# Release point of held outputs, buffers of the last batch and the order of the opening in a one-core attention-and-convolution kernel

## The chip, the cores and the metric

The kernel runs on one core of a Trainium2 chip. The metric is the device time of one execution in microseconds (us). The kernel before has three timed runs, 1046.08, 1042.27 and 1046.51 us, so a median of 1046.08 us, and one profiled execution of 1042.6 us.

## The reference, cut to what matters

```
# u, v: (8, 3136, 256)   z: (8, 3136, 64)   B, S, D = 8, 3136, 256
scores = z @ z.T / S
attn   = maximum(scores, 0) ** 2
x      = u * (attn @ v)
x1, x2, x3 = split(x @ w_proj)                       # three times 256 columns
conv   = irfft(rfft(x2, axis=1) * rfft(filter, axis=0), n=S, axis=1)
out    = (x1 * conv * x3) @ w_out
```

Inputs and output are float32. The convolution is circular, along the 3136 positions, each of 256 channels by itself.

## The kernel before, in words

**Tiles.** The 3136 positions are seen as 64 times 49 (N1 times N2). They make 25 tiles of 128 positions, the last half full, in seven chunks of 512, 384, 512, 384, 512, 384 and 448 positions (CHUNKS). The eight batches follow each other, seven chunks each.

**Attention.** For each pair of position tiles (a "unit") and each chunk, TensorE makes scores into PSUM (score_mm, L1335), ScalarE applies the relu (L1510), and the square is made by VectorE (L1519) or ScalarE (L1517), whichever the planner finds earlier. The weighing matmuls (L1365; L1472 for the half tile) multiply the squares by v and sum in PSUM. Scores are symmetric, so a square made for one chunk is also used for the next two: DMA transposes on SyncE's queue (L1450) write it to the tiles M, M2e, M2o. VectorE then multiplies by u (L1559), for which u comes in by GpSimd DMA and is transposed by SyncE's queue (L1196).

**Projection and convolution.** Each chunk is projected. Two products become a gate (L897, L909, L917), kept in SBUF; the third (L940) goes through the first part of a Fourier transform (dft1, L755) and is put to DRAM (D1, L762). When a batch has all its chunks there, its 16 lines are loaded (load_spec, L787), transformed (forward, L808 and L816), multiplied by the filter's spectrum H on VectorE (L1012), transformed back (inverse or inverse2), and put to DRAM again (D2, L1062). Then add_end loads each chunk (load_c, L799), does the last part (L1098, L1101), multiplies by the gate (L1104), by w_out (L1132), copies to an output tile (copy, L359 on ScalarE or L363 on VectorE) and stores it (L1160, two DMAs for a chunk).

**The end of the kernel.** In the last batch a load_spec brings two lines instead of four, and from a ring of two buffers (l_p). The four chunks 3 to 6 of batch 6 are held back (HOLD is 3): their ends are of the planner's lowest kind, FZ, and may start once the last square of batch 7 (q_) is made. Their inputs and three of their output tiles lie in memory that v's buffers leave (cut_in, cut_out). The ends of batch 7 go in the order FINAL (0, 2, 4, 6, 1, 3, 5) and write to R_p tiles (two buffers) for even chunks, then xh_p tiles (three buffers) for odd ones.

**The opening.** z of batch 0 is loaded in three pieces by SyncE's queue (L450, ten DMAs), cast twice side by side by VectorE or ScalarE (L363, L359), turned by TensorE (L551) and copied to zT. v comes by GpSimd's queue in three pieces (L418, L423). Small tables are made meanwhile, as one chain: constants per partition (percol, L590 to L595; percol2, L598 to L614, 17 instructions on 128x1), the table T1 (t1_first, sin_steps with lines L627, L628, L632, then a sine L635), its transpose (t4_pe, L660), and the table S2 (L678 to L685, then L695 to L703), with transposes of S2 (L717) at the end.

**What sets the order.** The kernel is scheduled by hand: a planner (class Plan) runs through a model of the engines with the costs that each task is given, and emits an instruction where its model starts it. Each engine's order, and each queue's, is then fixed. S (scores) come first; FA, W, FB and FZ fill the rest by credit. `after(task, at)` forbids the model to start a task before a time; ZF_AT, V_AT and U_AT are such times, for pieces of z, v and u. A dependence marked ISSUED orders only the model and adds no wait on the chip. So a changed time in the opening moves instructions in all eight batches.

Of the kernel before, what the change touches and what calls it, by code (L numbers as in the profile page):

```python
# [11 lines left out]
P = 128  # L12
F32 = mybir.dt.float32
BF16 = mybir.dt.bfloat16
# [229 lines left out]
def kernel(  # L244
# [108 lines left out]
    def on(engine, emit, cost, deps=(), takes=(), **kw):  # L353
        return job(None, lambda e: emit(), {engine: cost}, deps, takes, **kw)
# [117 lines left out]
    wp16 = const.tile([P, 2, 3 * D], BF16, name="wp16")  # L472
    nc.gpsimd.dma_start(out=wp16[:], in_=moe_w_proj.rearrange("(t p) n -> p t n", p=P))
    wo16 = const.tile([P, 2, D], BF16, name="wo16")
    ZF_AT, V_AT, U_AT = (4.5, 6.0, 7.0), (8.0, 15.0), (19.0, 22.0)

    def filt_row(i, n=1):
        t = filt[i // 8]
# [135 lines left out]
        nc.vector.tensor_scalar(half, half, -0.5, 1.0, ALU.mult, ALU.add)  # L614

    step("DVE", percol, 0.9)

    def sin_steps(box, w, first, dst=None, at=0.0):
        def a():
# [31 lines left out]
        nc.vector.tensor_scalar(m[:, N1 : N1 + 1], k1v[:, 0:1], n1p, pb, ALU.mult, ALU.add)  # L651

    t1_done, _ = sin_steps({}, P, t1_first, T1[:, :], 6.6)
    step("DVE", percol2, 2.6)

    box1 = {}

# [15 lines left out]
    for j0 in (0, 8):  # L673
        box = {}

        def first(m, j0=j0):
            if j0:
                nc.vector.scalar_tensor_tensor(php, tp, 8.0, php, ALU.mult, ALU.add)  # L678
            nc.vector.tensor_scalar(m[:, 0 : 8 * N2], k2v, tp, php, ALU.mult, ALU.add)

        def masks(j0=j0, box=box):
            v = box["v"][:KR, 0 : 8 * N2].rearrange("p (j k) -> p j k", k=N2)
            a = int(j0 == 0)
            nc.vector.tensor_scalar(S2[:KR, ds(3 + j0 + a, 8 - a), 0:N2], v[:, a:], r0[:KR], None, ALU.mult)
            nc.vector.tensor_scalar(S2[:KR, ds(3 + j0, 8), 50 : 50 + N2], v, r1[:KR], None, ALU.mult)  # L685

        _, ta = sin_steps(box, 8 * N2, first)
        t = step("DVE", masks, 0.8)
        t.frees.append((ta, 0))
        if j0 == 0:  # L690
            join(t, s2_zero)
        s2_done.append(t)
# [86 lines left out]
    def by_row(d):  # L779
        return d[0:S, :].rearrange("(p x) d -> p x d", x=2 * NJ)  # L780

    def load_spec(src, j0, nj, deps, late=0.0):
        box = {}

        def go():
            box["t"] = l_p.tile()
            nc.sync.dma_start(out=box["t"][:KR, 0 : 2 * nj, :], in_=by_row(src)[:, ds(2 * j0, 2 * nj), :])  # L787

        t = on("SP", go, 0.45, [*deps, *((d, ISSUED) for d in loads[-1:])], [l_p.slots], moves=0.6 * nj, late=late)
        return in_order(t), box  # L790

    def load_c(src, c, deps, home):
# [88 lines left out]
    def add_proj(b, c, xt, xt_tasks):  # L881
# [83 lines left out]
            to_spectrum()  # L965
        return users, puts, gtasks

    def add_spectrum(b, puts):
        deps0 = list(h_done) + list(tz_done) if b == 0 else []
        final = b == B - 1  # L970
# [4 lines left out]
        for g in range(NJ // 2):  # L975
            own = not final or g % 2 == 0
            xh, gh = (xh_p, gs_p) if own else (R_p, A_p)
            if 2 * g % per == 0:
                ldb[0] = load_spec(D1[b % 2], 2 * g, per, puts, LATE_LOAD * (not final))
            ld, ibox = ldb[0]  # L980
            ends_load = (2 * g + 2) % per == 0
            xb = {}
            evs = []
            firsts = []
            for i in range(2):
                j = 2 * g + i
                box = {}

                def mm(i=i, j=j, box=box, xb=xb, ibox=ibox, xh=xh):
                    box["p"] = bank()  # L990
                    if i == 0:
                        xb["x"] = xh.tile([P, 2, 4, D], BF16)
                    x = ibox["t"][:KR, ds(2 * (j % per), 2), :].rearrange("p c d -> p (c d)")
                    forward(box["p"], x, j)

                def ev(e, i=i, box=box, xb=xb):
                    copy(e, xb["x"][:KC, 0, ds(2 * i, 2), :].rearrange("p c d -> p (c d)"), box["p"][:KC, :])

                a = pe("FB", mm, c_line(j), [ld, *deps0, *firsts], [ps_m.slots, *([] if i else [xh.slots])])
                firsts = [a]  # L1000
                if i == 0:
                    a0 = a
                elif ends_load:
                    a.frees.append((ld, 0))
                e_ = job(None, ev, both(2 * D), [a])
                e_.frees.append((a, 0))
                evs.append(e_)

            def mul(i, g=g, xb=xb):
                x = xb["x"][:KC].rearrange("p i (j c) d -> p i j c d", c=2)  # L1010
                h = H[:KC, ds(2 * g, 2), i].unsqueeze(2).to_broadcast([KC, 2, 2, D])
                nc.vector.tensor_tensor(x[:, 1 - i], x[:, 0], h, ALU.mult)  # L1012

            def add(xb=xb):
                x = xb["x"][:KC].rearrange("p i (j c) d -> p i c j d", c=2)
                nc.vector.tensor_tensor(x[:, 1, 0], x[:, 1, 0], x[:, 0, 1], ALU.subtract)
                nc.vector.tensor_tensor(x[:, 1, 1], x[:, 1, 1], x[:, 0, 0], ALU.add)

            cost = c_dve2(4 * D)
            w_ = on("DVE", lambda mul=mul: mul(0), cost, evs, prio=ZP)  # L1020
            w_ = on("DVE", lambda mul=mul: mul(1), cost, [w_], prio=ZP, lat=ZL)
            z_ = w_ if final else on("DVE", add, 2 * c_dve2(2 * D), [w_], prio=ZP)

            def inv(g=g, xb=xb, z_=z_, a0=a0, gh=gh):
                if 2 * g % per == 0:
                    gb[0] = {"es": [], "firsts": []}
                gx = gb[0]
                for i in range(2):
                    j = 2 * g + i
                    box = {}  # L1030
                    new = j % per == 0

                    def mm(j=j, box=box, new=new):
                        box["p"] = bank()
                        if new:
                            gx["g"] = gh.tile([P, 2 * per, D], BF16)
                        z, y = (xb["x"][:KC, i, ds(j % 2 * 2, 2), :].rearrange("p c d -> p (c d)") for i in range(2))
                        if final:
                            inverse2(box["p"], y, z, j)
                        else:  # L1040
                            inverse(box["p"], y, j)

                    def ev(e, j=j, box=box):
                        copy(e, gx["g"][:KR, ds(2 * (j % per), 2), :].rearrange("p c d -> p (c d)"), box["p"][:KR, :])

                    a = pe(
                        "FB", mm, c_line(j) * (1 + final), [z_, *gx["firsts"], *(minus_task if final else [])], [ps_m.slots] + ([gh.slots] if new else [])
                    )
                    gx["firsts"] = [a]
                    if new:  # L1050
                        gx["g0"] = a
                    if i:
                        a.frees.append((a0, 1))
                    e_ = job(None, ev, both(2 * D), [a])
                    e_.frees.append((a, 0))
                    gx["es"].append(e_)
                if (2 * g + 2) % per:
                    return
                j0 = 2 * g + 2 - per

                def put():
                    nc.sync.dma_start(  # L1062
                        out=by_row(D2[b % 2])[:, ds(2 * j0, 2 * per), :], in_=gx["g"][:KR, 0 : 2 * per, :]
                    )

                p_ = on("SP", put, 0.4, gx["es"], moves=0.5 * per, late=LATE_D2 * (not final))
                p_.frees.append((gx["g0"], 1))
                lasts.append(p_)

            behind.append(inv)  # L1070
            if g >= SPEC_LAG:
                behind.pop(0)()
# [2 lines left out]
        return lasts  # L1075

    def add_end(b, lasts, gtasks, cs, kind="FB", src=c_p, dsts=(o_p,), late=0, behind=(), then=(), split=False):
        for c in cs:
            t0, nt = T0[c], len(tiles[c])
            w = CHUNKS[c]  # L1080
            dst = dsts[c % len(dsts)]
            ld, cb = load_c(D2[b % 2], c, lasts, src)
            yb = {}
            ys = []
# [289 lines left out]
    def add_weigh(un, data, done):  # L1374
        global_k = len(plans[un[:2]])

        def part(dhs):
# [6 lines left out]
                [ps_o[dh].slots for dh in dhs] if k == 0 else [],  # L1384
            )
            if b == 0 and c == 0:
                after(t, V_AT[0] if max(plans[b, c][k][1]) < 7 else V_AT[1])
            if 1 in dhs:
                done(t)
            if k == 0:  # L1390
# [86 lines left out]
    for gi, g in enumerate(groups):  # L1477
# [22 lines left out]
        for i, un in enumerate(g):  # L1500
# [22 lines left out]
                "ACT", relu, c_act(n * cw), [(st, -sum(costs[i + 1 :]) - extra)], [R_p.slots], prio=0  # L1523
            )
            r_.frees.append((st, i))
            q_ = job(None, sq, both(n * cw, "DVE"), [r_], [A_p.slots], prio=1)
            q_.frees.append((r_, 0))
            if c == NC - 1 and last or gi == len(groups) - 1:
                if b == 0:
# [14 lines left out]
            if last:  # L1544
# [24 lines left out]
                if c == NC - 1:  # L1569
# [7 lines left out]
                        held = lasts, gts  # L1577
                        held_w = w_
                    else:
                        add_end(b, lasts, gts, FINAL, "FB", A_p, (R_p, xh_p), split=True)  # L1580
                        early = [*held[0], held_w]
                        outs = (o_p, cut_out, cut_out, cut_out, o_p, o_p)
                        add_end(b - 1, early, held[1], range(HOLD, NC), "FZ", cut_in, outs, 4, [(loads[-1], ISSUED)], [q_])
                    if b == 0:
                        hold = Held(v_p.slots, v_slot[0])
                        w_.frees.append((hold, 0))
# [58 lines left out]
```

## Time and profile before

| what | us |
|---|---|
| profiled execution | 1042.6 |
| its span, first to last instruction | 1040.7 |
| around the span | 1.9 |
| TensorE busy in the span | 989.8 |
| ScalarE busy | 912.6 |
| VectorE busy | 819.1 |
| GpSimd busy | 190.4 |
| mean granted TensorE clock | 0.992 |
| DMA moved in the span | 167.99 MB |

A row of a timeline has the start, the length, the engine, the line in the kernel, the operation with output and inputs, how many instructions are merged, and in brackets how long the engine was idle before and what released it. A row of the windows view gives, for a stretch, the busy time and the number of instructions of TensorE (PE), its weight loads (PEld), VectorE (DVE), ScalarE (ACT) and GpSimd (POOL), then the granted clock, the mean busy share of the 16 DMA engines, and GB/s. Merged matmuls overlap: their length is the sum of the steps from start to start and the last one's own length.

### The profile page before, as it was taken

How to read it: one execution, taken by the hardware profiler on the slowest of the kernel's cores; microseconds unless marked ns; L12 is line 12 of the kernel's file. 1: busy time of each engine (PE TensorE's matmuls, PEld its weight loads, DVE VectorE, ACT ScalarE, POOL GpSimd, SP SyncE). 2: the span in 40 equal slices, each digit the busy share in tenths (PEclk: the TensorE clock that was granted, in tenths of full speed). 3: DMA queues.
4: the chain of work that ended last, by engine and by line, in shares of the span. 5: the costliest groups of instructions: out<-in, count | busy, mean ns of one | idle time of the engine just before them, and what ended most of it. 6: DMA issues, size and time to landing. Idle time of an engine off the chain costs nothing.

```text
span 1040.7 us, 17903 instructions
## 1 busy us (share of the span) xinstructions
PE 989.8 (95%) x6010; PEld 480.7 (46%) x6078; DVE 819.1 (79%) x1497; ACT 912.6 (88%) x1273; POOL 190.4 (18%) x401
## 2 busy tenths in 40 slices
PE   5999899999999999999999999999999999999974
PEld 2444444444444545445454454444544454444553
DVE  6867588977788768986879777997879968897673
ACT  6998799987999889997999889997989989999672
POOL 5033111311023300313021311121202230001000
PEclk9999999999999999999999999999999999999997
DMA  9599767888887868899888979798887977868357
GB/s 165 96 157 180 136 141 147 164 147 164 184 159 138 170 135 206 167 153 145 160 203 156 172 170 181 147 173 157 193 174 147 161 167 163 201 137 184 83 157 214
DMA packets 324380, 167.99 MB, mean 161 GB/s; under 512 B 234088, under 2 KB 302184, under 8 KB 324288
## 3 DMA queue, kind: packets, MB, share of 16 engines
q1 hardware_dynamic: 296560, 135.87, 59.7%
q0 software_dynamic: 27728, 30.97, 21.7%
q8 instruction: 48, 0.79, 0.3%
q14 instruction: 44, 0.36, 0.1%
HBM read 90.26 MB, written 53.35 MB: 138 GB/s over the span
## 4 chain that ended last, share of the span: by engine, by line
PE 75%; DVE 8%; ACT 7%; DMA 5%; issue 3%; SPq 1%; another core or an unknown queue 0%; ACTq 0%; DVEq 0%; POOL 0%; POOLq 0%
PE ps_o_t L1365 40%; PE ps_s_t L1335 11%; PE ps_m_t L940 4%; ACT R_t L1510 4%; PE ps_m_t L1132 4%; PE ps_m_t L909 3%; PE ps_m_t L897 3%; PE ps_m_t L755 2%; DMA M_t<-A_t 2%; PE ps_m_t L824 2%; PE ps_m_t L1101 2%; PE ps_m_t L816 2%; DVE xT_t L1559 2%; DVE A_t L1519 2%; ACT A_t L1517 1%
## 5 line engine op out<-in xcount | busy, mean ns | idle before, releaser
L1510 ACT ACTIVATE R_t<-ps_s_t 128x1024 f32<-128x1024 f32 (+2 forms) x552 | 485.0, 921 | 33.3 <-PE ps_s_t L1335 27.8
L1365 PE MATMUL ps_o_t<-A_t,v_t 128*128 128x512 bf16 (+2 forms) x2011 | 465.4, 354 | 3.6 <-issue 0.5
L1365 PEld LDWEIGHTS <-v_t 128*128 128x128 bf16 x2688 | 253.6, 98 | 241.6 <-issue 30.0
L1519 DVE TENSOR_TENSOR A_t<-R_t 128x768 bf16<-128x768 f32 (+2 forms) x271 | 290.7, 1080 | 35.2 <-ACT R_t L1510 29.4
L1517 ACT ACTIVATE A_t<-R_t 128x768 bf16<-128x768 f32 (+3 forms) x281 | 265.8, 958 | 5.4 <-DMA spec<-s_t 0.9
L1335 PE MATMUL ps_s_t<-zT_t 64*128 64x512 bf16 (+2 forms) x1088 | 155.3, 358 | 3.7 <-ACT R_t L1510 3.0
L408 POOL COPY tick<-xT_t 1x1 bf16<-1x1 bf16 x54 | 15.9, 294 | 737.5 <-DVE xT_t L1559 737.5
L1559 DVE SCALAR_TENSOR_TENSOR xT_t<-ps_o_t,uT_t 128x256 bf16<-128x256 f32 (+1 forms) x224 | 76.5, 383 | 29.1 <-PE ps_o_t L1365 18.4
L917 DVE TENSOR_TENSOR gate_t<-ps_m_t,x_t 128x256 bf16<-128x256 f32 (+1 forms) x208 | 69.0, 385 | 30.8 <-PE ps_m_t L909 15.1
L1365 PE MATMUL ps_o_t<-M_t,v_t 128*128 128x384 bf16 (+2 forms) x336 | 79.1, 346 | 6.7 <-DMA M_t<-A_t 6.6
L1012 DVE TENSOR_TENSOR xh<-xh,H 100x1024 bf16<-100x1024 bf16 x120 | 81.5, 684 | 2.3 <-ACT xh L359 1.4
L1335 PEld LDWEIGHTS <-zT_t 64*128 64x128 bf16 x1088 | 32.9, 94 | 101.8 <-issue 99.8
L359 ACT ACTIVATE x_t<-ps_m_t 128x512 bf16<-128x512 f32 (+3 forms) x114 | 61.7, 564 | 16.7 <-PE ps_m_t L897 12.2
L363 DVE CAST x_t<-ps_m_t 128x512 bf16<-128x512 f32 (+3 forms) x99 | 60.0, 621 | 15.6 <-PE ps_m_t L940 10.8
L1104 DVE TENSOR_TENSOR yT_t<-ps_m_t,gate_t 128x512 bf16<-128x512 f32 (+2 forms) x97 | 58.2, 619 | 16.3 <-PE ps_m_t L1101 12.5
L363 DVE CAST s_t<-ps_m_t 128x512 bf16<-128x512 f32 (+1 forms) x72 | 45.9, 644 | 25.9 <-PE ps_m_t L755 24.4
L399 POOL DMA_DIRECT2D un_t<-in_u_dram x112 | 60.0, 558 | 8.7 <-issue 6.5
L418 POOL DMA_DIRECT2D v_t<-in_v_dram x112 | 59.4, 555 | 4.6 <-issue 2.5
L940 PE MATMUL ps_m_t<-wp,xT_t 128*128 128x256 bf16 x396 | 57.6, 274 | 0.5 <-DVE gate_t L917 0.3
L1132 PE MATMUL ps_m_t<-wo,yT_t 128*128 128x256 bf16 (+1 forms) x348 | 54.9, 278 | 0.2
L897 PE MATMUL ps_m_t<-xT_t,wp 128*128 128x512 bf16 (+2 forms) x203 | 51.7, 353 | 2.0 <-DVE xT_t L1559 1.7
L1365 PE MATMUL ps_o_t<-M2e_t,v_t 128*128 128x512 bf16 (+1 forms) x192 | 51.7, 370 | 0.3 <-issue 0.2
(179 smaller groups left out, 961.7 us busy)
## 6 DMA issues: line engine op xcount, KB each, us to landing
out_dram<-ost_t SPq DMA_DIRECT2D x49, 256.0 KB
spec<-s_t SPq DMA_DIRECT2D x88, 128.0 KB
spec_in_t<-spec SPq DMA_DIRECT2D x28, 392.0 KB
spec<-gs_t SPq DMA_DIRECT2D x28, 392.0 KB
out_dram<-ost_t SPq DMA_DIRECT2D x47, 192.0 KB
v_t<-in_v_dram POOLq DMA_DIRECT2D x56, 128.0 KB, 4.3
un_t<-in_u_dram POOLq DMA_DIRECT2D x56, 128.0 KB, 5.1
conv_in_t<-spec SPq DMA_DIRECT2D x26, 256.0 KB
```

The source lines that it names most:

```text
L363: nc.vector.tensor_copy(out_, in_)
L897: nc.tensor.matmul(box["p"][:, :cw], wp16[:, k, ds(nb * P, P)], xt["t"][:, k, :cw], start=(k == 0), stop=(k == 1),)
L917: nc.vector.tensor_tensor(g[:, ::-1] if h == 0 else g, p, x, ALU.mult)
L940: nc.tensor.matmul(box["p"][:, ds(k_ * D, D)], xt["t"][:, k, ds((at + k_) * P, P)], wp16[:, k, ds(D, D)], start=(k == 0), stop=(k == 1),)
L1012: nc.vector.tensor_tensor(x[:, 1 - i], x[:, 0], h, ALU.mult)
L1132: nc.tensor.matmul(box["p"][:rows, ds(i * D, D)], yb["y"][:, k, ds((i0 + i) * P, rows)], wo16[:, k, :], start=(k == 0), stop=(k == 1),)
L1335: nc.tensor.matmul(ps[:m, i, :cw], zt[h, ds(t * P, m)], zt[h, ds(C0[c], cw)], start=True, stop=True)
L1365: nc.tensor.matmul(o, row(v16[b], t)[:, ds(dh * P, P)], x, start=(k == 0 and i == 0), stop=(last and i == len(pair) - 1),)
L1510: nc.scalar.activation(box["R"][:rows, 0:n, :cw], live[un][:rows, 0:n, :cw], AF.Relu)
L1517: nc.scalar.activation(a, r, AF.Square)
L1519: nc.vector.tensor_tensor(a, r, r, ALU.mult)
L1559: nc.vector.scalar_tensor_tensor(x, f, inv_s2, ut, ALU.mult, ALU.mult)
```

## The change

The opening. percol2 moves to directly behind percol, ahead of T1. S2's table may not start before 30 in the planner's time (S2_AT). The times for the three pieces of z become 4.7, 9.2 and 12.3; those for v become three steps (8.5 for tiles under 7, 12.5 for tiles under 14, 16.5 for the rest) in place of two (8.0 and 15.0). In the first chunk of batch 0, squares behind the second unit are given to VectorE alone.

The end. The held outputs may start once the last inverse matmul of batch 7 is issued. The last batch's load_spec takes its buffers in turn from l_p, c_p and un_p (six instead of two). Outputs of the last batch go to R, xh, gs, R, xh, gs, xh in the order in which they are made; those of the held chunks to three cut_out tiles and one o_p tile, where it was one cut_out and three o_p.

```
-    ZF_AT, V_AT, U_AT = (4.5, 6.0, 7.0), (8.0, 15.0), (19.0, 22.0)
+    S2_AT = 30.0
+    ZF_AT, V_AT, U_AT = (4.7, 9.2, 12.3), ((7, 8.5), (14, 12.5), (NT, 16.5)), (19.0, 22.0)
...
     step("DVE", percol, 0.9)
+    step("DVE", percol2, 2.6)
...
     t1_done, _ = sin_steps({}, P, t1_first, T1[:, :], 6.6)
-    step("DVE", percol2, 2.6)
...
-        _, ta = sin_steps(box, 8 * N2, first)
+        _, ta = sin_steps(box, 8 * N2, first, at=S2_AT)
...
-    def load_spec(src, j0, nj, deps, late=0.0):
+    def load_spec(src, j0, nj, deps, late=0.0, home=l_p):
         box = {}
 
         def go():
-            box["t"] = l_p.tile()
+            box["t"] = home.tile([P, 8, D] if home is l_p else [P, 4, D], BF16)
...
-        t = on("SP", go, 0.45, [*deps, *((d, ISSUED) for d in loads[-1:])], [l_p.slots], moves=0.6 * nj, late=late)
+        t = on("SP", go, 0.45, [*deps, *((d, ISSUED) for d in loads[-1:])], [home.slots], moves=0.6 * nj, late=late)
...
+    inverses = []
...
-                ldb[0] = load_spec(D1[b % 2], 2 * g, per, puts, LATE_LOAD * (not final))
+                ldb[0] = load_spec(D1[b % 2], 2 * g, per, puts, LATE_LOAD * (not final), (l_p, c_p, un_p)[g % 3] if final else l_p)
...
+                    inverses.append(a)
...
-        for c in cs:
+        for at, c in enumerate(cs):
...
-            dst = dsts[c % len(dsts)]
+            dst = dsts[at % len(dsts)]
...
-                after(t, V_AT[0] if max(plans[b, c][k][1]) < 7 else V_AT[1])
+                after(t, next(at for n_, at in V_AT if max(plans[b, c][k][1]) < n_))
...
-            q_ = job(None, sq, both(n * cw, "DVE"), [r_], [A_p.slots], prio=1)
+            how = {"DVE": c_dve(n * cw)} if (b, c) == (0, 0) and k > 1 else both(n * cw, "DVE")
+            q_ = job(None, sq, how, [r_], [A_p.slots], prio=1)
...
-                        add_end(b, lasts, gts, FINAL, "FB", A_p, (R_p, xh_p), split=True)
+                        add_end(b, lasts, gts, FINAL, "FB", A_p, (R_p, xh_p, gs_p, R_p, xh_p, gs_p, xh_p), split=True)
...
-                        outs = (o_p, cut_out, cut_out, cut_out, o_p, o_p)
-                        add_end(b - 1, early, held[1], range(HOLD, NC), "FZ", cut_in, outs, 4, [(loads[-1], ISSUED)], [q_])
+                        outs = (cut_out, cut_out, cut_out, o_p)
+                        add_end(b - 1, early, held[1], range(HOLD, NC), "FZ", cut_in, outs, 4, [(loads[-1], ISSUED)], [(inverses[-1], ISSUED)])
```

## The prediction

> **What bounds the kernel now.** First the page's slices, to see where TensorE is not full.
>
> ```profile
> PE   5999899999999999999999999999999999999974
> ...
> DMA  9599767888887868899888979798887977868357
> ```
>
> TensorE is full but for the first slice and the last two (26 us each). So a microsecond won at either end stays won, if the middle stays full. Then windows over both ends.
>
> ```profile
> 0.00:5.00 5.00, 0.00 (x0) 0.00 (x0) 1.22 (x10) 1.61 (x3) 4.24 (x17) 1.00 0.50 88
> 5.00:10.00 5.00, 1.64 (x8) 0.48 (x8) 1.34 (x4) 1.04 (x4) 4.32 (x9) 1.00 1.02 200
> 10.00:15.00 5.00, 2.70 (x23) 2.23 (x25) 3.69 (x15) 3.23 (x5) 3.21 (x7) 1.00 1.13 219
> ...
> 40.00:50.00 10.00, 10.00 (x81) 5.50 (x80) 8.24 (x17) 9.94 (x15) 0.00 (x0) 1.00 0.78 155
> 50.00:60.00 10.00, 9.84 (x58) 4.40 (x57) 7.76 (x15) 9.90 (x13) 3.48 (x7) 1.00 0.93 150
> 989.20:1012.50 23.30, 19.02 (x141) 13.65 (x142) 20.17 (x37) 16.44 (x32) 0.00 (x0) 1.00 0.47 144
> 1016.00:1024.00 8.00, 3.95 (x32) 3.17 (x33) 2.83 (x5) 0.98 (x2) 0.00 (x0) 0.55 0.95 254
> 1024.00:1039.00 15.00, 6.76 (x71) 5.24 (x68) 5.44 (x10) 6.01 (x14) 0.00 (x0) 0.93 0.74 217
> 1026.00:1028.00 2.00, 1.53 (x16) 1.09 (x15) 1.33 (x3) 0.00 (x0) 0.00 (x0) 1.00 0.99 283
> 1036.00:1038.00 2.00, 0.00 (x0) 0.00 (x0) 0.00 (x0) 0.00 (x0) 0.00 (x0) 0.71 0.89 295
> ```
>
> The reader sees: up to 10, no engine but GpSimd works, and DMA is full with z and v; 36 to 60 is full on ScalarE; the last spectrum (989.2 to 1012.5) is VectorE's, 20.17 of 23.3; behind it DMA is the busiest. Third, TensorE's rows where the opening and the last spectrum end, and where work resumes.
>
> ```profile
> 27.64 1.90 PE L1365 MATMUL ps_o_t<-A_t,v_t 128*128 128x512 bf16 x8
> ...
> 33.55 1.89 PE L1365 MATMUL ps_o_t<-A_t,v_t 128*128 128x512 bf16 x7 [0.22 <-DVE A_t L1519]
> ...
> 1012.25 0.38 PE L808 MATMUL ps_o_t<-R_t,TZ 100*98 100x256 bf16 x2
> ...
> 1019.63 1.03 PE L1101 MATMUL ps_s_t<-T,A_t 128*128 128x128 bf16 x8 [5.57 <-DMA A_t<-spec]
> ```
>
> Chunk (0,0) is done at 35.4 (33.55 + 1.89), the last inverse at 1012.6. The chain of waits says what fills the gap behind it and what stops the tail:
>
> ```profile
> 1013.35 2.85 DMA spec<-A_t
> ...
> 1016.69 4.34 DMA A_t<-spec
> ...
> 1026.09 3.71 DMA out_dram<-R_t
> ```
>
> Last, TensorE's waits from 40 to 985:
>
> ```profile
> PE ps_o_t L1365 <- DMA M_t<-A_t: 6.6, 4, 2.3
> ```
>
> **Opening.** percol2's 17 instructions take 2.5 us at 18.71 to 21.2; moved to 2.6 they end at 5.1, before the first turned z (6.0), where VectorE was idle: free. T1's steps run at 6.8 to 8.6, between pieces of z (landing at 4.9, 9.25 and 12.44), also free. The price: both casts of piece 1 go to ScalarE, so its matmuls start 0.35 later (5.7 for 5.35). The first relu needs no longer wait behind piece 2's casts (9.99 becomes 7.5), the first weighing comes at 9.9 instead of 15.72.
>
> From 16 on, VectorE has only squares: 9 of 1024 and one of 512 for chunk 0. A square row is 1.22 long, 1.14 from start to start; 9 x 1.14 + 0.6 = 10.9, so 26.9. ScalarE has relus alone, 0.97 each, and keeps ahead. TensorE has 42 weighing matmuls from 15.3 on (step (1.90 - 0.38) / 7 = 0.216, so 9.1) and seven score groups (about 0.45, 3.2): 27.6 at best. The last eight weighings (1.9) follow the last square: 28.8; I take 29.5, 0.7 for waits. Chunk 0 ends 5.9 earlier than 35.4.
>
> Given back: the two halves of S2 (2.5 each in VectorE's rows at 23 to 34; their sines 1.1 on ScalarE) now fall between 30 and 60. There, from 40 to 60, ScalarE has 0.16 idle and VectorE 4.0; S2's last part (1.8) and the copies to TZ (1.7) lay there before and now come later. What does not fit keeps TensorE waiting: from 0.5 to all 5.9; I take 1.5, since VectorE's idle row covers most of the 5.0. SyncE's transposes keep their order and start with the earlier squares; GpSimd's order is the same up to its 361st instruction. **Opening: -4.4 (0 to -5.4).**
>
> A row speaks against an early T1: L627 on 128x128 took 1.45 at 15.62, beside GpSimd's memset (16.07 to 16.98), where the same line on 392 columns takes 0.36 at 24.98. T1's steps now run beside GpSimd's issues of v (4.81 to 8.98); a second such row costs 1.1, inside the range. The Trainium skill (GPSIMD Engine Reference, Specifications) says that GpSimd and VectorE share their SBUF interfaces; the trace agrees by that 1.45, and by the rule alone the opening would be -3.3.
>
> **Middle.** The planner's order shifts in all batches. What I can price is the last chunk's wait for M, four times: 1.5 (at 120.8), 2.1 (246.2), 2.25 (370.6), 0.7 (495.3), the 6.6 above. I counted matmul columns between chunk 5's last score and chunk 6's first M weighing, in both orders, at 0.216 per 512. Before, batches 0 to 6: 18.8, 19.6, 20.9, 20.2, 21.7, 20.6, 22.6 us; the first four waited. Changed: 19.4, 21.7, 21.7, 21.5, 20.6, 21.7, 21.3. Batch 0 should still wait about 1; the others mostly not. That would be -5; transposes queue behind two chunk loads on SyncE now, so I take **-3** (-6.6 to +5).
>
> **End.** Six buffers let six spectrum loads go at once (before: two, then each behind a forward matmul). The held chunks' work leaves the spectrum: all its matmuls come behind the last inverse in the new order. VectorE then has 4 casts, 16 multiplies and 4 gate halves from 990.3 on: 4 x 0.6 + 16 x 0.605 + 4 x 0.32 = 13.4, then 0.85 for two inverses: 1004.5. ScalarE has 30 copies of 0.49 = 14.7 from 989.9: also 1004.6. Two full engines in lockstep lose some: last inverse T at 1005.5 (1004.5 to 1007.5), for 1012.6: 7.1 earlier.
>
> Behind T the held chunks' VectorE work (8 x 0.52 = 4.1) and ScalarE copies (3.6) fit into the gap of 7 us that stays (put 2.85, load 3.4, first at T + 7.6): hidden. Final outputs wait for no store now. But bytes move with it. From T + 3.1 on DMA has the held stores 1.77 MB, chunk loads 1.64 and final stores 3.21: 6.62 MB. Loads at 254 GB/s (1016 to 1024) 6.5 us; stores at 285, between the rows 283 and 295, 17.5. Computing needs only about T + 19, so DMA sets the end: 3.1 + 24.0, and 1.7 from the last byte (1039.0) to the span's end: T + 28.8 = 1034.3 for 1040.7. **End: -6.4**; bounds below.
>
> **Sum.** 1042.6 - 4.4 - 3 - 6.4 = 1028.8 against the profiled execution. Its own time lies 3.5 below the median of the runs (1046.08; they spread over 4.2), so timed runs of the changed kernel may lie 0 to 3.5 above; with 2.2, **1031**.
>
> **Rivals.**
> 1. *Stores drain slower.* From 1016 to 1039 the tail moved 254 x 8 + 217 x 15 = 5.3 MB, 230 GB/s. If that is what DMA gives and not the stall on R (3.71 above), 6.62 MB take 28.8 us: T + 33.6, end -1.6, total 1036. For: it is what the tail did. Against: a share of 0.74 in most of it, and 0.99 with 283 where stores were queued.
> 2. *Tables come back whole.* ScalarE is full from 40 to 60; S2 on VectorE pushes squares to it, and all 5.9 are lost: opening 0, total 1035.4. Against: VectorE's 4.0 idle.
> 3. *Stores drain faster.* 295 at share 0.89 is 331 at full share: 20 us for all, T + 24.8, 1027. The Trainium skill (DMA: Bandwidth & Descriptors, Specifications) gives about 358 GB/s of HBM for a core; by it the tail would be 18.5 us. Here only 370.6 to 371.2, 0.6 us, lies above it (398).
> 4. *Slower.* Every turnover waits for M as batch 2 did: 2.25 idle, and behind it the clock at half for 3.3 us:
>
> ```profile
> 371.30:374.60 3.30, 3.30 (x15) 1.13 (x13) 0.69 (x1) 0.78 (x1) 0.00 (x0) 0.50 0.21 61
> ```
>
> that is 2.25 + 1.65 = 3.9, seven times 27.3 for 6.55 + 1.65 = 8.2 before: 19.1 in place of the -3, total 1053. From 2.9 per turnover on it outweighs both ends, from 3.6 on by over 0.5%. Against: six of seven leads are over 20.5.
> 5. *It does not do what it says:* held outputs still in the spectrum. ISSUED adds no wait, only an order. Then the end gains nothing: 1037. Against: in the new order every held matmul stands behind the last inverse.
>
> **Chances.** Forecast 0.62 (1024 to 1038), rival 1 0.16, 2 0.10, 3 0.06, 4 0.04, 5 0.02. The range reaches to rival 1 with a late T (1041) and to rival 3 with the middle's best: 1022 to 1041. A measurement of this kernel tells about 0.5% from no change, so 1040.9 and 1051.3. Faster: 0.60 + 0.12 + 0.08 + 0.06 = 0.86; the rest of the first three and rival 5, 0.10, the same; slower 0.04.
>
> **What would show it.** Right: the first weighing near 10 and chunk 0 done near 29.5; TensorE still over 9.8 of 10 from 36 to 60; under 3 us of waits for M; the last inverse at 16 us from the first forward matmul; the held matmuls directly behind it; DMA share over 0.9 from there to the end, and last copies some 8 us before it. Wrong: idle TensorE at 36 to 60 with ScalarE full (2); DMA share 0.95 with under 240 GB/s (1); M waits at every turnover (4); DMA share under 0.8 in the tail, which would mean that something else than bytes sets the end.

## The result and the profile after

The changed kernel takes **1033.26 us** (median of four runs, 1031.16 to 1036.37), the kernel before 1045.95 (four runs, 1042.27 to 1046.51): a ratio of 0.9897, 95% interval 0.9872 to 0.9921, so some 10.8 us faster by the ratio; the medians lie 12.7 apart. The profiled execution took 1032.26 with a span of 1030.0, for 1042.6 and 1040.7. Gains in this document go by the ratios, which can differ in the third place from a quotient of medians (0.9879 here).

The page's slices of the kernel after:

```profile
PE   6999899999999999999999999999999999999984
...
DMA  9799857898878989798878988798887877967448
```

The windows that answer to those of before, and one more at 110 to 130. The last row is that same window in the kernel before:

```profile
5.00:10.00 5.00, 2.67 (x13) 0.69 (x11) 4.55 (x15) 3.44 (x5) 4.32 (x9) 1.00 0.99 199
10.00:15.00 5.00, 4.88 (x36) 2.29 (x35) 3.82 (x13) 2.41 (x3) 3.37 (x8) 1.00 1.15 224
40.00:50.00 10.00, 10.00 (x61) 4.63 (x63) 9.26 (x21) 9.94 (x14) 3.47 (x7) 1.00 0.81 143
110.00:130.00 20.00, 15.54 (x84) 7.20 (x83) 9.74 (x20) 14.62 (x20) 3.37 (x7) 1.00 0.83 154
1010.00:1015.00 5.00, 4.93 (x55) 3.87 (x53) 4.49 (x8) 3.57 (x6) 0.00 (x0) 1.00 1.08 357
1015.00:1020.00 5.00, 3.90 (x38) 2.55 (x36) 2.76 (x6) 3.79 (x9) 0.00 (x0) 1.00 0.88 290
1020.00:1025.00 5.00, 0.00 (x0) 0.00 (x0) 0.00 (x0) 0.07 (x1) 0.00 (x0) 0.69 0.86 263
...
110.00:130.00 20.00, 16.84 (x95) 7.97 (x95) 9.99 (x20) 13.17 (x19) 4.32 (x9) 1.00 0.74 142
```

TensorE now works 4.88 of the 5 us from 10 on (2.70 before), and 40 to 50 is still full. The hole at 110 to 130 has grown: 4.46 us of idle TensorE for 3.16, of which 1.5 were the wait for M at 120.8. In the tail the DMA share is 0.86 or more from 1010 to 1025, but only 0.74 from 1002 to 1010. TensorE's rows:

```profile
27.50 1.89 PE L1369 MATMUL ps_o_t<-A_t,v_t 128*128 128x512 bf16 x8
...
984.34 0.64 PE L809 MATMUL ps_s_t<-spec_in_t,S 98*100 98x256 bf16 x4 [1.38 <-DMA spec_in_t<-spec]
...
1000.50 0.38 PE L809 MATMUL ps_m_t<-R_t,TZ 100*98 100x256 bf16 x2
...
1008.37 0.40 PE L1105 MATMUL ps_s_t<-T,A_t 128*128 128x128 bf16 x4 [1.21 <-DMA A_t<-spec]
```

Chunk (0,0) is done at 29.4 (35.4 before). The last spectrum's first forward matmul comes at 984.3 (989.2), the last inverse ends at T = 1000.9 (1012.6): 16.5 us behind it for 23.4. The first final chunk comes at T + 7.5; the span ends at T + 29.1 (28.1).

So **the 10.7 us of span come from two places**: 6.9 from the spectrum less 1.0 in the tail, and 4.9 at 984. How the 4.9 came about is seen first from the x evictions (the last step of a chunk's attention, L1559 of before, L1564 of after). In VectorE's rows that of chunk (0,4) ends at 98.5 before and 94.1 after, 4.5 earlier; that of (0,6), the last of batch 0, ends at the same time. First before, then after:

```profile
130.69 0.68 DVE L1559 SCALAR_TENSOR_TENSOR xT_t<-ps_o_t,uT_t 128x256 bf16<-128x256 f32 x2
```

```profile
130.75 0.68 DVE L1564 SCALAR_TENSOR_TENSOR xT_t<-ps_o_t,uT_t 128x256 bf16<-128x256 f32 x2
```

That last mark is not a fair one. By then the changed kernel has already run 16 of the 19 forward matmuls of the filter's own spectrum (3.0 us), and the kernel before none; its first comes at 139.0. First before, then after:

```profile
139.03 0.60 PE L808 MATMUL ps_m_t<-spec_in_t,S 98*100 98x256 bf16 x4
```

```profile
120.62 0.60 PE L809 MATMUL ps_m_t<-spec_in_t,S 98*100 98x256 bf16 x4 [1.90 <-DMA spec_in_t<-specf]
```

A count of all matmuls that TensorE has started by a given time is fairer (0.216 us for 512 columns, as in the prediction). The profile of before lacks 68 of its 6078 matmul records, so there it goes by the weight loads, one to a matmul, with the lengths of e2_end, which keeps the order of before up to 988. By this count after is ahead of before by 5.6 us at 80, 4.4 at 105, 2.4 at 131, 1.8 at 150, 8.1 at 500 and 5.8 at 980. Of the opening's 6 us some 4 are thus lost within batch 0, most of it between 105 and 150, and about 2 stay. TensorE's waits between 40 and 985 and the chain of waits between 105 and 130 name a cause:

```profile
PE ps_m_t L809 <- DMA spec_in_t<-specf: 1.9, 1, 1.9
...
PE ps_o_t L1369 <- DMA M_t<-A_t: 1.1, 1, 1.1
PE ps_m_t L817 <- DMA spec_in_t<-specf: 1.1, 1, 1.1
```

```profile
110.69 2.15 SPq L1454
...
112.94 7.63 DMA spec_in_t<-specf
...
122.85 4.03 DMA spec_in_t<-specf
```

These are the first and the third of the four loads of the filter's own spectrum (load_spec on DF), needed once. The first is issued behind two transposes into M on SyncE's queue and lands 7.6 us later. The third goes out at 122.85, when forward matmuls have freed one of the two buffers, and lands 4.0 us later. In the new order the first forward matmul stands at 109.4 us of the count above (124.0 in the old one), so TensorE waits for both. The wait for M, 6.6 before, is 1.1: that is where batches 1 to 3 get back some 5 us. From 500 on a part of the lead, 8.1 to 5.8, is lost again, and no experiment says where.

### The profile page after: what moved, and what is told of

The parts are those of the page before. It is cut to its first block, busy times and chain, and to the rows that moved or that the text cites. A ratio compares the mean times of both kernels' runs of the same rounds, so it can differ in the third digit from the quotient of the medians.

```text
span 1030.0 us, 17937 instructions
## 1 busy us (share of the span) xinstructions
PE 991.5 (96%) x6078; PEld 478.1 (46%) x6078; DVE 822.7 (80%) x1484; ACT 912.3 (89%) x1286; POOL 184.5 (18%) x401
## 2 busy tenths in 40 slices
DMA packets 324379, 167.98 MB, mean 163 GB/s; under 512 B 234088, under 2 KB 302184, under 8 KB 324288
## 4 chain that ended last, share of the span: by engine, by line
PE 74%; DVE 8%; DMA 7%; ACT 6%; issue 3%; SPq 2%; ACTq 0%; DVEq 0%
PE ps_o_t L1369 38%; PE ps_s_t L1339 11%; PE ps_m_t L941 4%; PE ps_m_t L1136 4%; PE ps_m_t L910 4%; PE ps_m_t L898 3%; PE ps_m_t L756 3%; ACT R_t L1514 2%; DVE A_t L1523 2%; PE ps_m_t L1105 2%; DVE xT_t L1564 2%; PE ps_m_t L817 2%; PE ps_m_t L825 2%; DVE xh L1015 2%; ACT A_t L1521 1%
## 5 line engine op out<-in xcount | busy, mean ns | idle before, releaser
L1369 PE MATMUL ps_o_t<-A_t,v_t 128*128 128x512 bf16 (+2 forms) x2064 | 470.2, 354 | 1.2 <-DVE A_t L1523 0.9
L1523 DVE TENSOR_TENSOR A_t<-R_t 128x1024 bf16<-128x1024 f32 (+2 forms) x295 | 316.5, 1080 | 38.4 <-ACT R_t L1514 27.9
L1521 ACT ACTIVATE A_t<-R_t 128x1024 bf16<-128x1024 f32 (+2 forms) x257 | 241.9, 950 | 10.3 <-issue 2.2
L408 POOL COPY tick<-xT_t 1x1 bf16<-1x1 bf16 x54 | 9.8, 182 | 737.9 <-DVE xT_t L1564 737.9
L1564 DVE SCALAR_TENSOR_TENSOR xT_t<-ps_o_t,uT_t 128x256 bf16<-128x256 f32 (+1 forms) x224 | 76.5, 383 | 29.0 <-PE ps_o_t L1369 23.4
L359 ACT ACTIVATE x_t<-ps_m_t 128x512 bf16<-128x512 f32 (+3 forms) x131 | 70.2, 565 | 26.0 <-PE ps_m_t L898 15.7
L1108 DVE TENSOR_TENSOR yT_t<-ps_m_t,gate_t 128x512 bf16<-128x512 f32 (+2 forms) x98 | 59.1, 620 | 16.5 <-PE ps_m_t L1105 12.8
L363 DVE CAST x_t<-ps_m_t 128x512 bf16<-128x512 f32 (+3 forms) x81 | 48.7, 618 | 13.3 <-PE ps_m_t L941 8.2
L359 ACT ACTIVATE xh<-ps_m_t 100x512 bf16<-100x512 f32 (+1 forms) x91 | 54.2, 615 | 2.2 <-PE ps_m_t L817 1.3
L363 DVE CAST s_t<-ps_m_t 128x512 bf16<-128x512 f32 (+1 forms) x67 | 41.7, 631 | 15.1 <-PE ps_m_t L756 14.2
L1136 PE MATMUL ps_m_t<-wo,yT_t 128*128 128x256 bf16 (+1 forms) x346 | 52.7, 274 | 0.3 <-DVE yT_t L1108 0.3
```

The source lines that it names most:

```text
L359: nc.scalar.activation(out_, in_, AF.Copy)
L363: nc.vector.tensor_copy(out_, in_)
L1136: nc.tensor.matmul(box["p"][:rows, ds(i * D, D)], yb["y"][:, k, ds((i0 + i) * P, rows)], wo16[:, k, :], start=(k == 0), stop=(k == 1),)
L1369: nc.tensor.matmul(o, row(v16[b], t)[:, ds(dh * P, P)], x, start=(k == 0 and i == 0), stop=(last and i == len(pair) - 1),)
L1521: nc.scalar.activation(a, r, AF.Square)
L1523: nc.vector.tensor_tensor(a, r, r, ALU.mult)
```

## The experiments

All ran beside the kernel before. T - t0 is the last spectrum, from its first forward matmul to the end of the last inverse; the tail is from there to the span's end; both are of the profiled execution. A difference between two ratios of this table has a half-width of 3 to 4.5 us.

| run | ratio to before (95%) | median us | t0 | T - t0 | tail |
|---|---|---|---|---|---|
| before | 1 | 1045.95 | 989.2 | 23.4 | 28.1 |
| after | 0.9897 (0.9872 to 0.9921) | 1033.26 | 984.3 | 16.5 | 29.1 |
| e1_open | 0.9981 (0.9965 to 0.9998) | 1043.17 | 987.6 | 24.2 | 30.0 |
| e2_end | 0.9928 (0.9907 to 0.9950) | 1038.46 | 992.1 | 17.5 | 28.0 |
| e3_spec_late | 0.9872 (0.9850 to 0.9893) | 1032.05 | 985.5 | 16.3 | 27.8 |
| e4_no_store | 0.9895 (0.9876 to 0.9914) | 1034.04 | 988.0 | 17.4 | 25.5 |
| e5_rel_old | 0.9934 (0.9910 to 0.9959) | 1038.13 | 987.5 | 19.8 | 28.6 |
| e6_home_old | 0.9991 (0.9976 to 1.0007) | 1044.15 | 987.6 | 26.1 | 28.0 |
| e7_no_held | 0.9862 (0.9840 to 0.9883) | 1030.42 | 984.9 | 17.5 | 25.3 |
| e8_act_store | 0.9909 (0.9885 to 0.9933) | 1034.40 | 986.1 | 16.0 | 30.8 |
| e9_s2_early | 0.9943 (0.9921 to 0.9964) | 1037.68 | 994.8 | 16.1 | 28.2 |
| e10_dst_old | 0.9940 (0.9923 to 0.9958) | 1036.12 | 983.9 | 18.2 | 31.7 |
| e11_late_o3 | 0.9850 (0.9824 to 0.9876) | 1027.03 | 983.0 | 15.7 | 29.0 |
| e12_o3 | 0.9881 (0.9846 to 0.9916) | 1032.05 | 985.0 | 16.0 | 28.4 |

A warning on t0: after, e1, e4, e5, e6, e7, e8 and e10 have one and the same order on TensorE up to the last spectrum, and their t0 lies between 983.9 and 988.0. TensorE's idle time around the turnover of batch 2 (340 to 380) alone goes from 0 to 2.3 us among them. A single profiled t0 is no better than that. The end varies too: the six kernels that have the whole new end unaltered (after, e2, e3, e9, e11, e12) have T - t0 from 15.7 to 17.5 and tails from 27.8 to 29.1, of which after's is the longest.

**e1_open: the opening alone.** after.py's opening with before's end (its release, homes and outputs).

> The opening alone, with the end of before (its order on TensorE and SyncE is that of after up to the last spectrum). Theory: the opening wins 6 us up to 35 us, its gain shrinks to about 4.5 by chunk 4 of batch 0, is all lost at 110 to 130 us behind the loads of the filter's spectrum, and 5 us come back later because the waits for M fall from 6.6 to about 1: so -5 in time (1041), the last x evictions of batch 0 level with before and those of batch 6 about 5 earlier, and M waits under 2 us. Rival 1 (my prediction's terms as they stood, opening -4.4 and middle -3): -7.4 (1038.5), with batch 0 ending 4 us earlier than before. Rival 2: the loss in batch 0 and the gain in the middle are chance of one execution: 0 to -3 and another picture.

Measured: -2.0 us (0.9981 of 1046; interval -3.7 to -0.2). The x evictions follow the theory: chunk (0,4) 3.7 earlier, (0,6) 0.4 earlier, (6,6) 3.7 earlier. M waits are 0.2. But TensorE waits 1.6 for a store of an output tile at the turnover of batch 2 (the passage to the next batch), and this execution's end is 2.7 longer than before's (24.2 + 30.0 against 51.5), with the clock at half for 17.1 us from 1009.3 on where before has 10.2. Rival 1 is out. The picture is the theory's but for the count, by which 2.2 us of lead are left at 150; the size is that of rival 2 (0 to -3), so how much of the middle's gain is chance stays open.

**e2_end: the end alone.** before.py with after's release, homes and outputs.

> The end alone, with the opening of before (its order is that of before up to 989 us of matmul columns, so the whole middle is that of before). Theory: last inverse 16.5 us behind the first forward matmul of the last spectrum for 23.4, tail of 29 us for 28: -6 in time (1040). The two parts lie in different orders and add up: this and the opening alone together give the -12.7 of after. Rival 1: the tail is bound by bytes from a fixed rate of 230 GB/s: -1.6 (1044.5). Rival 2: the two parts need each other (the end gains by the clock or buffers that the opening leaves): their sum differs from that of after by more than 2 us.

Measured: -7.5 us (-9.7 to -5.2). T - t0 is 17.5 with a tail of 28.0, while M waits are 7.0 as before. 0.9981 times 0.9928 is 0.9909, near the 0.9897 of both: the parts add up within the intervals. **The end is most of the change.**

**e3_spec_late: the filter's loads planned later.**

```
-        ld, ibox = load_spec(DF, j0, 4, puts)
+        ld, ibox = load_spec(DF, j0, 4, puts, 6.0)
```

> After, with the landing of the filter's spectrum loads planned 6 us later, which moves their forward matmuls back in TensorE's order (the order is the same up to 109 us). Theory: TensorE's waits for these loads (1.9 and 1.1 us in after) and most of the 3.0 that ScalarE waits behind them go, batch 0 ends 3 us earlier than in after, and the time is 3 us below it (1030), if the waits for M do not come back. Rival: those matmuls only fill what TensorE has to wait for anyway (M, x), so batch 0 ends where it does now and the time is that of after (1033).

Measured: the waits for specf are gone, and the last x evictions of batch 0 end 3.5 us earlier than in after, as the theory says. Only 11 of the forward matmuls lie ahead of that mark here; by the count of matmuls this kernel is 4.5 us ahead of before at 80 and still 3.8 at 150, where after fell from 5.6 to 1.8. VectorE's row:

```profile
127.20 0.68 DVE L1564 SCALAR_TENSOR_TENSOR xT_t<-ps_o_t,uT_t 128x256 bf16<-128x256 f32 x2
```

The time gains less: 0.9872 for 0.9897, with intervals that overlap, so the time alone does not rule out the rival. At 362 a part is lost again: TensorE waits for an output tile whose store has not landed, and then runs at half clock (waits and windows of this kernel):

```profile
PE ps_m_t L1105 <- DMA out_dram<-ost_t: 2.8, 1, 2.8
```

```profile
360.00:365.00 5.00, 2.96 (x18) 1.48 (x16) 2.02 (x3) 1.56 (x3) 0.15 (x1) 1.00 1.25 188
365.00:370.00 5.00, 4.24 (x26) 2.05 (x26) 1.79 (x4) 4.44 (x7) 0.00 (x0) 0.66 0.44 154
```

**e4_no_store: held chunks stored in part.** For kind FZ each store writes one tile instead of up to four.

> After, with most of the held chunks' outputs not stored (of each piece of a held chunk only one tile is written: the outputs of chunks 3 to 6 of batch 6 are left out for the most part); the matmuls and the copies stay, as does the order on TensorE. Theory (bytes set the tail's end): some 1.2 of 6.62 MB less, at 285 GB/s 4 us less (1029). Rival 1 (computing, or the chain put, load, matmul, copy sets the end): 0 (1033). Rival 2 (SyncE's issues set it, 0.5 to 1.5 us each): less than 1 us, since the number of stores stays.

Measured: DMA moved 1.51 MB less (166.47 for 167.98). The tail is 25.5, which is 3.6 shorter, but this execution's t0 was late, and the timed runs show no gain (0.9895 for 0.9897). By the tail bytes count, by the time they do not; e7 goes further.

**e5_rel_old: the old release.**

```
-... [(loads[-1], ISSUED)], [(inverses[-1], ISSUED)])
+... [(loads[-1], ISSUED)], [q_])
```

> After, with the held chunks' matmuls released as before (behind the last square of batch 6 instead of behind the last inverse); the order on TensorE is that of after up to the last spectrum, and then the held matmuls stand among those of the spectrum again. Theory (the end's gain comes from the held work leaving VectorE and ScalarE in the spectrum): the last inverse again 21 to 23 us behind the first forward matmul for 16.5, the tail 2 us shorter or the same: +4 to +6 against after (1038). Rival (the gain comes from six loads at once and from outputs that wait for no store): last inverse at 17 to 18 us, time within 1.5 us of after.

Measured: +3.9 against after (0.9934 - 0.9897, times 1046). Here T - t0 is 19.8, 3.3 more; behind T TensorE then has nothing to do, and its wait for the first final load is

```profile
PE ps_m_t L1105 <- DMA A_t<-spec: 7.3, 1, 7.3
```

for 1.21 in after. The clock is at half from 1010.1 on for 10.2 us. The size is near that of the theory, but the spectrum gives only half of what it expected, and its tail is no longer than after's (28.6 for 29.1), although TensorE stands idle there.

**e6_home_old: the last spectrum's loads in one pool again.**

```
-... LATE_LOAD * (not final), (l_p, c_p, un_p)[g % 3] if final else l_p)
+... LATE_LOAD * (not final), l_p)
```

> After, with the last spectrum's loads all in one pool again (fewer can be under way; the later ones wait for forward matmuls of earlier groups). Theory: the loads are a small part of the end: last inverse 17 to 18.5 us behind the first forward matmul for 16.5, time +0.5 to +2 (1035). Rival (the loads carry the end's gain): last inverse at 20 us or later, time +3.5 and more.

Measured: T - t0 is 26.1 and the time 0.9991: **the whole gain of the end is gone.** My theory fell, the rival holds and more. SyncE issues the eight loads in pairs, the first at 984.8, the next at 988.9, 994.8 and 1001.7, each later pair behind the forward matmuls of earlier groups; in after the last of the eight goes out at 986.4. The windows of this kernel, in steps of 3.41 us and cut 0.2 us behind the changes of the clock:

```profile
993.53:996.94 3.41, 1.63 (x10) 0.81 (x7) 3.36 (x6) 1.94 (x4) 0.00 (x0) 0.97 0.44 112
996.94:1000.35 3.41, 2.97 (x14) 2.87 (x15) 0.99 (x2) 1.54 (x3) 0.00 (x0) 0.50 0.34 123
...
1007.18:1010.60 3.42, 2.49 (x9) 1.18 (x8) 2.76 (x5) 1.68 (x3) 0.00 (x0) 0.50 0.35 108
1010.60:1014.01 3.41, 3.41 (x21) 3.21 (x20) 1.04 (x2) 2.01 (x4) 0.00 (x0) 0.53 0.15 41
```

With the held work out of the spectrum and loads in pairs, TensorE is idle for half of a window (1.63 of 3.41), the clock falls to half, and stays there for 17.1 us, while VectorE and ScalarE wait for the slow matmuls. How much of the 9.6 us the later loads cost by themselves, and how much the clock, no run separates. The Trainium skill (TensorE: Matmul & The Clock Gate, What's actually happening) has the clock judged in free-running windows of about 3.4 us; the trace agrees by these steps. The same section of the Trainium skill says that the clock falls after an idle window; here one that was busy for about half (1.63 of 3.41 in the row) was enough, and the longest idle in it was 1.33.

**e7_no_held: no store of the held chunks at all.** The store of kind FZ writes nothing.

> After, with no store at all of the held chunks (the outputs of chunks 3 to 6 of batch 6 are left out: 1.77 MB and 8 of SyncE's 22 issues in the tail), same order on TensorE. With most of their bytes away the tail was 26.6 us behind the last inverse for 29.1. Bytes as forecast (285 GB/s): -6.2 in the tail. Theory now: the tail is set partly by the bytes and partly by the compute chain, whose last copy lies 19.2 behind the last inverse and needs its own stores, landing and exit, some 5 us: so the tail is 24 to 25.5 us, 4 to 5 less, time -3 to -5 (1029). Rival (neither bytes nor issues set the end): the tail stays over 28 us.

Measured: tail 25.3, 3.8 shorter than after's and 2.5 shorter than the shortest tail with these stores, and 0.9862, 3.7 us below after, with a half-width of 3.4. The theory's size. But 8 of SyncE's issues are gone with the bytes, so this is not the price of the bytes alone. At 285 GB/s 1.77 MB would be 6.2: DMA isn't busy all through the tail (0.54 from 1002 to 1010), and the last copy, at T + 18.5 for 19.2, comes only 0.7 earlier without the stores.

**e8_act_store: three final chunks' stores issued by ScalarE.**

```
+            by = "ACT" if split and at in (2, 4, 6) else "SP"
```

> After, with the stores of three of the last five final chunks issued by ScalarE instead of SyncE; bytes and TensorE's order up to 1010 us of matmul columns are the same. If SyncE's issues (0.5 to 1.5 us each, 22 stores back to back from 1009 to 1027) set the end: 8 fewer of them, 4 to 5 us less in the tail (24 to 25). If bytes set it, as forecast: 0 (28.5 to 29.5), and the remaining issues only come later or take longer.

Measured: tail 30.8, time 0.9909. No gain, but the test is not clean: two issues hold ScalarE for 1.4 to 1.5 us, and its last copy ends at T + 22.1 for 19.2. Rows of ScalarE's queue:

```profile
1017.91 1.42 ACTq L1167 DMA_DIRECT2D out_dram<-gs_t  x2
...
1022.00 1.52 ACTq L1167 DMA_DIRECT2D out_dram<-xh  x2
```

So whether SyncE's issues alone cost something stays open.

**e9_s2_early: the tables not held back.** S2_AT is 0.0.

> After, with the tables S2 not held back (their sines and VectorE's rows stand in the opening again, as early as their inputs allow). Theory (the tables late are what lets chunk 0's squares run one behind the other, and cost little where they go): the last weighing of chunk (0,0) ends at 32 to 35 us for 29.4, and TensorE from 36 to 60 has nothing of it back but what the tables cost there, up to 1.5; batch 0's chunk 4 ends 2 to 4 us later than in after. By the end of batch 0 part of this is gone, since the filter's loads are late anyway: time +0 to +3 against after. Rival (the tables cost the same wherever they stand): chunk (0,0) ends later, but chunk 4 level with after.

Measured: the last weighing of chunk (0,0) ends at 31.7 for 29.4. VectorE's tables stand between the squares again:

```profile
21.71 0.15 DVE L679 SCALAR_TENSOR_TENSOR percol<-percol 128x1 f32<-128x1 f32 x1
...
22.82 0.37 DVE L630 TENSOR_SCALAR gs_t<-gs_t 128x392 f32<-128x392 f32 x1
23.10 2.35 DVE L1523 TENSOR_TENSOR A_t<-R_t 128x1024 bf16<-128x1024 f32 x2
```

Chunk (0,4) ends 2.6 later than in after, and later than in all seven others of after's order, so the tables do not cost the same wherever they stand: the rival is out. The time is +4.8 against after, more than expected. But the order of all batches moved with it (M waits 3.2 again, a stop at the end of batch 0 with half clock, t0 994.8), so this +4.8 is not the tables' price.

**e10_dst_old: the outputs' buffers of before.** `dsts[c % len(dsts)]`, with (R_p, xh_p) and the old six places.

> After, with the output buffers of before (final chunks in two rings instead of three, held ones over six places). Theory: with fewer buffers the final chunks' matmuls wait for stores in the tail, the last copy moves from 19.5 to 21 to 23 us behind the last inverse, and the tail grows by 1 to 3; T itself stays at 16 to 17 behind the first forward matmul: time +1 to +3. Rival (bytes alone set the tail's end): last copy later, tail and time the same.

Measured: last copy at T + 26.2 for 19.2, tail 31.7 for 29.1, time +4.5 against after (0.9940), T - t0 18.2. With the same bytes the tail is 2.6 longer, so bytes alone do not set it, and the rival is out. The theory's cause is seen once: ScalarE waits 2.5 us for a store before it can copy into an output tile. But the time is above its +1 to +3, T came later than it said, and TensorE ran at half clock from 1008.7 on for 6.8 us, which it did not foresee; the 2.6 is not the buffers' alone.

**e11_late_o3 and e12_o3: a third output buffer,** with and without the later loads.

```
-    o_p = Pool("ost", 2, [P, 4, D], F32)
+    o_p = Pool("ost", 3, [P, 4, D], F32)
...
-        ld, ibox = load_spec(DF, j0, 4, puts)
+        ld, ibox = load_spec(DF, j0, 4, puts, 6.0)
```

> After, with the filter's spectrum loads planned 6 us later and a third output buffer. With the late loads alone batch 0 won its 3.5 us, but TensorE waited 2.8 us at 363 us for a store of an output buffer, and the clock fell to half behind it. Theory: with a third buffer that wait goes, the turnover of batch 2 costs nothing, and the time is 3 us or more below after (1027 to 1030). Rival (another wait takes its place at that turnover, for the loads of D2 or M): 1031 to 1033.

> After, with a third output buffer alone; the filter's spectrum loads are planned as in after. Beside the late loads the third buffer gave 1027. Theory (the two gains add up: 3 us for the loads, 2 to 3 for the buffer): TensorE waits for the filter's loads as in after (2 to 3 us in all), the turnover of batch 2 runs without a stop, and the time is 1029.5 to 1031.5. Rival 1 (the buffer alone made the gain): 1027 to 1028. Rival 2 (the buffer only matters where the late loads have moved the turnover): 1033.

Measured: both together 1027.03, 0.9850. Against after that is 0.9953 (0.9850 / 0.9897), half-width 0.0036 from the two intervals: **4.9 us faster than the changed kernel.** The two windows that matter:

```profile
110.00:130.00 20.00, 18.17 (x105) 8.73 (x104) 9.73 (x22) 13.68 (x19) 4.32 (x9) 1.00 0.84 156
...
360.00:365.00 5.00, 5.00 (x35) 2.63 (x32) 3.50 (x7) 4.48 (x8) 1.86 (x4) 1.00 1.14 159
```

TensorE works 18.17 for 15.54, and there is no stop at 362. The opening has no share in what this execution shows: its clock was at half from 28.8 to 35.6, and chunk (0,4) ends 0.6 later than in before. Alone, the buffer gives 0.9881 and the loads 0.9872; -1.7 and -2.6 add to -4.3, near -4.9, as e12's theory has it. But neither step is clear of noise by itself (half-widths of 4.5 and 3.4), and e12's 1032.05 lies outside the theory's 1029.5 to 1031.5, nearer to the 1033 of rival 2, by which the buffer only matters beside the late loads. That both together help is shown; how the 4.9 divide is not.

## Why the prediction was right or wrong

The time lay 2.3 us above the forecast and in the range. By its steps:

- **Opening at its place: right.** percol2 ran free at 2.5 to 5.0, T1's steps at 5.7 to 7.8 (0.23 and 0.35 for L629 and L630; no second row of 1.45). The first weighing came at 8.98 (forecast 9.9), chunk 0 was done at 29.4 (29.5): -6.0.
- **"Given back ... I take 1.5": right up to chunk 4 of batch 0** (-4.5 left), with TensorE full from 36 to 60. **"Opening: -4.4" as a gain that lasts was too large by more than half.** By the count of matmuls 1.8 us are left at 150 in after, and 1.1 to 3.5 in the other seven executions of this order. The step that failed took the middle to be full because TensorE's slices were 9. An earlier batch 0 also moves everything that hangs on it: the planner put the filter's forward matmuls 14.6 us of columns earlier. It reckons a load of four lines, with nothing ahead of it, at 4.85 us from issue to landing (0.45, 1.2, four times 0.6, and 0.8); the first one landed after 7.6. e3 takes this away, and 3.8 us of lead are left at 150. I had compared both orders for M, not for these loads.
- **"Middle: -3" had the right mechanism; its size came out partly by luck.** M waits fell from 6.6 to 1.1 (0 to 1.7 in other executions of this order): -5.5. Of the -4.9 at t0, -1.8 was there at 150, which leaves -3.1. By the count, the lead gained between 150 and 980 is 4.0 in after and 0 to 3.2 in the seven others. Opening and middle together were forecast at -7.4. The profiled t0 gives -4.9, e1 -2.0 (-3.7 to -0.2).
- **"End: -6.4" was right in size:** -5.9 in the profile, -7.5 (-9.7 to -5.2) alone in e2. T - t0 was forecast at 16.3 and is 16.5; the held matmuls stand right behind T; final loads came at T + 7.5 (7.6). Its reasons were of unequal weight. I named six loads first but priced only VectorE's and ScalarE's work. The loads are the condition: without them the whole gain goes (e6); there the release leaves TensorE idle until the clock falls, and the loads come late as well. With them the release is worth 3.3 in the spectrum; filling the gap behind T made the tail no shorter (e5).
- **The tail, T + 28.8 forecast, 29.1 measured: right number, half the reason.** "DMA sets the end" holds in part: 1.77 MB and 8 issues less save 3.8, not 6.2 (e7), and the DMA share forecast at over 0.9 was 0.74 from 1002 to 1010 and 0.88 and 0.86 behind 1015. Buffers set it as well, as "final outputs wait for no store now" had it: 2.6 us, a stretch at half clock among them (e10).
- **The rivals.** 1, slower stores: out, T + 29.1 with 357 to 263 GB/s. 2, tables come back whole: out, 40 to 60 stayed full; the opening lost its gain later and elsewhere. 3, faster stores: out by the tail's length, though stores alone moved 371 GB/s for 1.5 us. 4, M at every turnover: out, one wait. 5: out.

So the forecast was 1028.8 against the profiled execution, which took 1032.3: an opening priced 2.6 too well, a middle 0.1 too badly, an end 0.5 too well, and 0.4 more around the span (2.3 for 1.9). The 2.2 added for the median were 1.0 in the result; this hid part of the miss.

## What to carry to other kernels

A gain in the first batch is only won if what comes due next is early too: look in both orders for every load that is needed once (here the filter's), and compare its place in the queue with the moment at which the new order asks for it. Compare two orders by the work done at a time and not by one mark such as the last eviction: work that moved across the mark hides what was won. Before taking work out of a stage to free one engine, ask what keeps TensorE busy there then: in e6, where the loads came two at a time, the clock fell and all that the end had won was lost. The planner reckoned at 4.85 us a load that took 7.6 behind transposes. That one landing time and the buffer that runs short next (e11) were together worth 4.9 us, almost half as much as the whole change.

## What the runs showed of the hardware

- The granted clock changes in steps of 3.41 us. In e6_home_old it fell after a step with TensorE busy for about half (1.63 of 3.41) and came back only after a full one; steps with 2.97 and 2.49 at half clock left it down. But the busy share of one step does not settle it in these runs. In before a step with 2.99 brought the clock back at 1023.2, and in after one with 1.51, on the same grid of steps, left it at full:

```profile
1019.77:1023.18 3.41, 2.99 (x22) 2.34 (x21) 2.15 (x4) 0.55 (x1) 0.00 (x0) 0.50 0.98 274
```

```profile
117.32:120.73 3.41, 1.51 (x10) 0.74 (x9) 0.00 (x0) 0.89 (x2) 0.00 (x0) 1.00 1.13 255
```

- Near 1012 to 1016, where the last chunk loads give way to stores, DMA moved up to 404 GB/s in slices of 0.75 us (the DMA view of after from 1000 to 1030):

```profile
GB/s 0 128 295 194 169 27 158 279 120 268 290 250 275 283 295 313 389 404 397 386 355 329 295 268 268 279 224 262 229 257 295 296 217 311 291 280 210 87 0 0
```

The loads' packets of 512 bytes end with the 19th slice. The next two (1014.25 to 1015.75) are stores alone, and moved 371 GB/s at a share of 1.02; apart from 40 packets under 512 bytes, all are of 2 KB and more:

```profile
DMA packets 199, 0.56 MB, mean 371 GB/s; under 512 B 40, under 2 KB 40, under 8 KB 199
```

From the 24th slice on (1017) the rate stayed between 210 and 311 until the stores ran out, at a share of 0.85 (1017.25 to 1027). The Trainium skill (DMA: Bandwidth & Descriptors, Specifications) gives about 358 GB/s of HBM for a core; the Trainium skill (Perfetto Trace Analysis, Roofline) lets a core that is alone go beyond it, up to some 435. The trace, with 404 in a slice, agrees with the second.
- Eight executions of one and the same order up to 984 differ by up to 4.1 us there, and TensorE's idle time at a single turnover (batch 2) differs by up to 2.3.
